# Attention and a gated layer on one core: one more slice of the second block in the shared stretch, and another order in the two pairs behind it

## The chip, the cores and the metric

The kernel runs on one core of a Trainium2 chip. The metric is the device time of one execution in microseconds (us), the median of three runs. Engines are named as in the profile: PE is TensorE, DVE is VectorE, ACT is ScalarE, POOL is GpSimd, SP is SyncE, whose queue issues nearly all DMAs here.

## The reference, cut to what matters

```python
def _attn_ref(q, k, v, n_global, n_local):          # q, k, v: (4, 8, 768, 64)
    scores = scale * np.matmul(q, k.transpose(0, 1, 3, 2))
    is_global = pos[None, :] < int(n_global)         # 8
    is_local = (rel >= 0) & (rel < int(n_local))     # 96
    keep = is_global | is_local
...
    scores = scores + bias[None, :, :, :]            # - slope of the head * distance
    scores = np.where(keep, scores, -1000000000.0)
    a = np.exp(scores - max); a = a / (sum + 1e-09)
    return np.matmul(a, v)

def _moe_ref(x, w_in, w_out):                        # x: (3072, 512), d_ff 2048
    h = x @ w_in
    g = h * np.clip(h + 3.0, 0.0, 6.0) / 6.0
    return g @ w_out
```

Attention with a band of 96 keys and 8 global ones gives x, 3072 tokens of 512 features; a gated layer follows. Both are computed in fp32 quality: a matrix is split into a high part and a rest (names with h and l: xh, xl, w1h, w1l), and three products are added.

## The kernel before, in words

The 3072 tokens are eight blocks of 384 (TB), numbered from 0. A block needs four pairs of heads, so pairs 0 to 3 belong to block 0, pairs 4 to 7 to block 1, and pairs 8 to 11 to block 2; pair 12 is the first of block 3. The gated layer of a block is cut into 16 slices of d_ff (f = 0 to 15). A slice is a first layer of 12 matmuls into a bank hp (L165), a gate (L176 on ACT, L177 on DVE), a high part gh (L185 on ACT, or L183 on POOL), the rest gl (L190 on DVE), and a second layer of 9 matmuls (L197). Block 0 sums its second layers in banks called acc, block 1 in banks called sp, tp and xp, which tells the two apart in the rows of L197.

`halves` (L433) writes these slices in a software pipeline: first layer of a slice, then the second layer of the slice before it, and after each of these two it yields, so that other work (a list of `units`) can be put between. One such first or second layer is called a half below. `finish` (L469) is the second layer that is still owed.

The weights come as 64-bit floats, and DVE decodes them, 32 chunks in all: chunk 2f gives w1 of slice f, chunk 2f+1 gives w2. In `decode` (L381) a chunk takes rows L393, L394, L402, L408 and L399 on DVE; the last, L399, writes w1l or w2l. ACT writes w1h or w2h just ahead of it (L412).

The program has these stretches:

- Attention of pairs 0 to 9 with the first three slices of block 0 at its end.
- The shared stretch (L568): slices of block 0, each of which needs two more chunks to be decoded, and slices of block 1, whose weights are there already, in the order of the string ORDER, one digit a slice (0 or 1 is the block). Where a slice's chunk is not decoded, `decoded_to` (L428) writes the missing decode steps into the program; `work` (L415) spreads the others by a count of PE and DVE time.
- The two moved pairs (L579): the rest of block 1's slices, with pairs 10 and 11 in the units between their halves. A pair's steps are `split` 0 to 2 (q and k into high part and rest: q1 on ACT, kx L783 on POOL, q L786 and kx L789 on DVE), `scores` of three tiles on PE (L812) with weights by exponentials behind them on DVE and ACT (L823, L827), `sum_up` (L837, L838 on DVE), `normalize` (L847 on POOL), `spread` (32x32 transposes L872 on DVE, then a DMA to a place in DRAM called there, L874), `fetch` (four DMAs from there into weights, L881), and `values` (20 matmuls L899 on PE, then xh on ACT and xl on DVE). Pair 11's `split` 2 and the like also issue the load of the pair two further on (L290).
- The layers of blocks 2 to 7, each with the pairs of the next block in its units.

`in_order` (L605) fixes the order on PE, SP and POOL as written; on DVE and ACT a scheduler may move rows a little. The tiles n and the buffers blocks exist three and two times, so a third `spread` waits until the DMA of the first has landed.

Of the kernel before, what the change touches and what calls it, by code (L numbers as in the profile page):

```python
# [20 lines left out]
NT = 3  # L21
TB = NT * P
NTB = S // TB
NPAIR = H // 2
NKT = DM // P
NF = DF // P
# [16 lines left out]
EARLY = 10  # L43
# [2 lines left out]
LEAD = 6  # L46
WAKE = 9
FIRST = 3
ORDER = "101001010010010100100"

def store(nc, pool, out, row, acc, last=False):
    for tt in range(NT):
# [5 lines left out]
class Kernel:  # L58
# [420 lines left out]
    def banded(self, flag):  # L479
# [12 lines left out]
        with ExitStack() as early, ExitStack() as words:  # L492
            x0 = self.x_tiles(self.pool("x0", 1, ctx=early, side="right"))
            xs = [x0, self.x_tiles(), self.x_tiles()]
# [8 lines left out]
            with ExitStack() as ctx:  # L503
# [7 lines left out]
                pairs = [Pair(self, n, xs[n // NPAIR], True) for n in range(EARLY)]  # L511
# [55 lines left out]
            next_f, todo = [FIRST, 0], []  # L567
            for block in map(int, ORDER):  # L568
                todo.append((block, next_f[block], xs[block], (acc, acc1)[block]))
# [6 lines left out]
        self.there = self.pool("there", 2, bass.MemoryType.DRAM)  # L576
        self.op = self.pool("op", 3, side="right")
        self.stage = "one"
        units, ahead = self.attention(2, xs[2], Pair(self, EARLY, xs[2], False), True)  # L579
        for k, _ in enumerate(self.halves([(1, f, xs[1], acc1) for f in range(next_f[1], NF)], True)):  # L580
            for unit in units[k]:
                unit()
        self.stage = "layers"
        x = xs[2]
        for i in range(2, len(self.blocks)):
            units, x_next = [], None
            if i + 1 < len(self.blocks):
                x_next = self.x_tiles()
                units, ahead = self.attention(i + 1, x_next, ahead)
                if i == 2:  # L590
                    units = [[]] + units
            else:
                units = [[]] * 4 + [[lambda: self.doubt(flag)]]
            acc = self.acc_tiles()
            steps = [(i, f, x, acc) for f in range(NF)]
            for k, _ in enumerate(self.halves(steps if x_next else steps[:-3], True)):
                for unit in units[k] if k < len(units) else ():
                    unit()
            if not x_next:
                self.end(steps[-3:])  # L600
            x = x_next
# [10 lines left out]
                        mybir.DependencyClass.NoSync, mybir.DependencyReason.DATA), reason="in_order")  # L612
                last[i.engine] = i.name

    def attention(self, i, x, first, begin=False):

        units = [[] for _ in range(2 * NF - 2)]
        pairs = [first]
        first.x = x
        if begin:  # L620
            for k in range(3):
                first.split(k, False)
            units[1].append(lambda: self.load_next(first.n, False))
        for n in range(first.n, (i + 1) * NPAIR):
            p = n - first.n
            me, after = pairs[p], Pair(self, n + 1, x, False) if n + 1 < len(self.blocks) * NPAIR else None
            pairs.append(after)
            at = units[5 * p + 1 if begin else 6 * p:]
            for t in range(NT):
                at[t].append(lambda t=t, me=me: me.scores(t)())  # L630
            if after:
                at[2 if begin else 3].append(lambda after=after: after.split(0))
            at[3] += [me.sum_up, lambda me=me: me.normalize(0), lambda me=me: me.normalize(1)]
            at[4] += [lambda me=me: me.normalize(2), lambda me=me: me.spread(0)]
            at[5] += [lambda me=me: me.spread(1), lambda me=me: me.spread(2), me.fetch]
            for t in range(1, NT if after else 0):
                at[t + (2 if begin else 3)].append(lambda t=t, after=after: after.split(t))
            if n % 2 == 1:
                at[9 if begin else 11] += [lambda me=pairs[p - 1]: me.values("x"), lambda me=me: me.values("s")]
        return units, pairs[-1]  # L640


    def general_setup(self):
# [109 lines left out]
class Pair:  # L753
# [136 lines left out]
    def values(self, bank="x"):  # L890
        nc, kk = self.nc, self.k
        _, _, va, vb = kk.loaded(self.n)
        xps = kk.bank(bank)[:, 0:TB]
        for t in range(NT):
            two = not self.low(t)
            for c in range(2 if two else 1):
                for j in range(2):
                    vt, K = (va, P) if c == 0 else (vb, CB)
                    nc.tensor.matmul(xps[j * D:(j + 1) * D, t * P:(t + 1) * P], lhsT=vt[0:K, t, j * D:(j + 1) * D],  # L899
                                     rhs=self.part(t, j, c, K), start=(c == 0), stop=(c == 1 or not two))  # L900
        kk.put_x(self.x, self.pr, xps)
        kk.load_next(self.n, True)
# [76 lines left out]
```

## Time and profile before

| what | value |
|---|---|
| median of three runs | 672.0 us (670.7 to 673.57) |
| the profiled execution, its own time | 672.15 us |
| span of its instructions | 670.3 us |
| DMA moved in it | 87.36 MB, mean 130 GB/s |
| mean granted TensorE clock | 0.997 of full speed |

The profile names a row by engine, source line and the tiles that it writes and reads; times are us from the start of the span. A busy PE is one with at least one matmul under way: matmuls overlap, so their single durations add up to more than the time they take. The granted clock (PEclk) is the share of full speed that the throttle let through. "Waited for" rows give the idle time of an engine just before an instruction, and what ended it.

### The profile page before, as it was taken

The numbers are of one execution on the slowest core, as the hardware profiler recorded it, in microseconds if no ns is written. First come the engines' busy times: TensorE is split into PE (matmuls) and PEld (weight loads), VectorE is DVE, ScalarE is ACT, GpSimd is POOL, SyncE is SP. The second block draws the span as 40 slices with busy tenths as digits, with TensorE's granted clock in tenths as the row PEclk, the third lists the DMA queues.
The fourth block names the chain that finished last, engine by engine and source line by source line (L and its number), as shares of the span: only waits on it lengthen the run. The fifth ranks groups of instructions, "written<-read, shape, count | busy, mean of one in ns | idle before, by whom it ended". The sixth has DMA issues, their size and how long they took to land.

```text
span 670.3 us, 11482 instructions
## 1 busy us (share of the span) xinstructions
PE 653.7 (98%) x3943; PEld 582.6 (87%) x3943; DVE 433.5 (65%) x1139; ACT 274.9 (41%) x726; POOL 221.0 (33%) x401
## 2 busy tenths in 40 slices
PE   9989999999998999999999999999999999999997
PEld 7768888887987999899999999899999999989995
DVE  6899999997663776457663787457762677422222
ACT  6897556554424333143423443143331444231111
POOL 5664222211340453134340453315441444302110
PEclk9999999998999999999999999999999999999999
DMA  8675544341464366625654267524555255510001
GB/s 296 180 212 176 166 142 151 132 157 33 129 164 123 93 175 181 175 73 138 166 139 134 87 165 193 156 94 119 150 158 142 80 149 142 142 48 1 1 1 53
DMA packets 65158, 87.36 MB, mean 130 GB/s; under 512 B 9665, under 2 KB 49857, under 8 KB 65089
## 3 DMA queue, kind: packets, MB, share of 16 engines
q1 hardware_dynamic: 64800, 86.26, 44.8%
q8 instruction: 33, 0.54, 0.3%
q14 instruction: 37, 0.29, 0.2%
q10 hardware_dynamic: 288, 0.26, 0.1%
HBM read 64.23 MB, written 22.28 MB: 129 GB/s over the span
## 4 chain that ended last, share of the span: by engine, by line
PE 75%; DVE 11%; DMA 5%; ACT 3%; issue 3%; POOL 1%; SPq 0%; ACTq 0%; POOLq 0%; DVEq 0%
PE hp L165 33%; PE acc L197 31%; DMA wst<-w 4%; PE tp L812 2%; PE xp L899 2%; DVE wz L402 2%; PE sp L899 2%; DVE wz L408 2%; PE sp L812 2%; ACT n L827 1%; DVE wz L394 1%; DVE wz L393 1%; DVE n L823 1%; DMA there<-blocks 1%; DVE w1l L399 1%
## 5 line engine op out<-in xcount | busy, mean ns | idle before, releaser
L176 ACT ACTIVATE g<-hp,small 128x384 f32<-128x384 f32 x127 | 73.7, 580 | 250.8 <-PE hp L165 224.0
L165 PE MATMUL hp<-xh,w1h 128*128 128x384 f32 x512 | 174.8, 341 | 1.3 <-ACT w1h L412 1.2
L165 PE MATMUL hp<-xh,w1l 128*128 128x384 f32 x512 | 173.7, 339 | 1.4 <-DVE w1l L399 1.4
L165 PE MATMUL hp<-xl,w1h 128*128 128x384 f32 x512 | 172.6, 337 | 0.0
L183 POOL TENSOR_SCALAR gh<-g 128x384 fp32r<-128x384 f32 x104 | 56.1, 539 | 316.5 <-DVE g L177 280.7
L197 PE MATMUL acc<-w2h,gl 128*128 128x512 f32 x336 | 133.2, 396 | 0.2
L197 PE MATMUL acc<-w2l,gh 128*128 128x512 f32 x336 | 132.5, 394 | 0.0
L197 PE MATMUL acc<-w2h,gh 128*128 128x512 f32 x336 | 132.4, 394 | 0.1
L177 DVE SCALAR_TENSOR_TENSOR g<-g,hp 128x384 f32<-128x384 f32 x128 | 69.5, 543 | 69.3 <-ACT g L176 68.9
L190 DVE TENSOR_TENSOR gl<-g,gh 128x384 fp32r<-128x384 f32 x128 | 81.2, 634 | 48.4 <-POOL gh L183 48.4
L847 POOL TENSOR_SCALAR n<-n,sums 128x232 f32<-128x232 f32 (+1 forms) x186 | 98.8, 549 | 35.8 <-DVE sums L838 22.0
L827 ACT ACTIVATE n<-n,least 128x232 f32<-128x232 f32 (+1 forms) x192 | 89.1, 466 | 46.0 <-DVE least L823 44.6
L165 PEld LDWEIGHTS hp<-xh,w1h 128*128 128x128 f32 x512 | 96.6, 189 | 7.9 <-ACT w1h L412 2.2
L165 PEld LDWEIGHTS hp<-xl,w1h 128*128 128x128 f32 x512 | 96.6, 189 | 3.7
L165 PEld LDWEIGHTS hp<-xh,w1l 128*128 128x128 f32 x512 | 96.5, 188 | 2.4 <-DVE w1l L399 2.4
L197 PEld LDWEIGHTS acc<-w2h,gl 128*128 128x128 f32 x336 | 63.1, 188 | 16.1 <-DVE gl L190 2.6
L197 PEld LDWEIGHTS acc<-w2h,gh 128*128 128x128 f32 x336 | 63.4, 189 | 10.6 <-ACT gh L185 0.4
L197 PEld LDWEIGHTS acc<-w2l,gh 128*128 128x128 f32 x336 | 63.3, 188 | 10.3
L872 DVE STREAM_TRANSPOSE blocks<-n 128x256 f32<-128x256 f32 x122 | 47.5, 424 | 30.7 <-POOL n L847 18.2
L375 POOL TENSOR_SCALAR we<-wst 128x512 int32<-128x512 uint32 x32 | 24.5, 766 | 77.0 <-DMA wst<-w 68.4
L823 DVE CUSTOM_DVE_ANT_0 n<-tp,d 128x232 f32<-128x232 f32 (+1 forms) x70 | 23.7, 375 | 31.6 <-PE tp L812 31.3
L783 POOL TENSOR_SCALAR kx<-load 64x504 fp32r<-64x504 f32 (+1 forms) x44 | 34.0, 774 | 8.0 <-PE hp L165 5.7
(117 smaller groups left out, 768.2 us busy)
## 6 DMA issues: line engine op xcount, KB each, us to landing
wst<-w SPq DMA_DIRECT2D x32, 512.0 KB, 3.5
there<-blocks SPq DMA_DIRECT2D x56, 256.0 KB, 2.6
load<-pairs SPq DMA_DIRECT2D x22, 636.0 KB, 5.4
load<-pairs SPq DMA_DIRECT2D x32, 384.0 KB, 4.2
weights<-there SPq DMA_DIRECT2D x48, 192.0 KB, 3.8
weights<-there SPq DMA_DIRECT2D x40, 160.0 KB, 3.4
out<-o SPq DMA_DIRECT2D x23, 256.0 KB, 2.1
load<-pairs SPq DMA_DIRECT2D x9, 444.0 KB, 3.8
```

Source lines behind the costliest of these rows:

```text
L165: self.nc.tensor.matmul(hp, lhsT=self.w1(w, f)[:, kt, :], rhs=a[:, kt, :], start=(n == 0), stop=(n == 3 * NKT - 1))
L176: nc.scalar.activation(out=g, in_=hp, func=AF.Relu, bias=self.three, scale=1.0)
L177: nc.vector.scalar_tensor_tensor(out=g, in0=g, scalar=6.0, in1=hp, op0=ALU.min, op1=ALU.mult)
L183: self.nc.gpsimd.tensor_scalar(out=gh, in0=g, scalar1=1.0, scalar2=0.0, op0=ALU.mult, op1=ALU.add)
L190: self.nc.vector.tensor_tensor(out=gl, in0=g, in1=gh.bitcast(F32), op=ALU.subtract)
L197: self.nc.tensor.matmul(acc[tt], lhsT=a[:, tk], rhs=self.w2(w, f), start=(f == 0 and j == 0), stop=(f == NF - 1 and j == 2))
L783: nc.gpsimd.tensor_scalar(out=part["kx"][own, c], in0=k[own, c], scalar1=1.0, scalar2=0.0, op0=ALU.mult, op1=ALU.add)
L812: nc.tensor.matmul(sp[j][:, lo:W], lhsT=q[:, t], rhs=part["kx"][:, c], start=(m == 0), stop=(m == 1))
L823: nc.vector.tensor_tensor_reduce(out=e[:, j, lo:W], in0=sp[j][:, lo:W], in1=d, op0=ALU.add, op1=ALU.min, scale=scale, scalar=3.0e38, accum ...
L827: nc.scalar.activation(out=e[:, j, lo:W], in_=e[:, j, lo:W], func=AF.Exp, bias=self.least[:, i:i + 1], scale=-1.0, accum_out=self.sums[:, ...
L847: nc.gpsimd.tensor_scalar(out=e[:, j, lo:W], in0=e[:, j, lo:W], scalar1=over, scalar2=0.0, op0=ALU.mult, op1=ALU.add)
L872: nc.vector.transpose(out=blocks[:, :, s].rearrange("p b j q -> p j b q"), in_=e[:, :, c:c + P].rearrange("p j (b q) -> p j b q", b=4))
```

## The change: what it does

```diff
-ORDER = "101001010010010100100"
+ORDER = "1010010100101001010010"
...
-        units, ahead = self.attention(2, xs[2], Pair(self, EARLY, xs[2], False), True)
+        units, values, ahead = self.two_pairs(xs[2])
         for k, _ in enumerate(self.halves([(1, f, xs[1], acc1) for f in range(next_f[1], NF)], True)):
             for unit in units[k]:
                 unit()
+        self.finish()
+        values()
...
-                if i == 2:
-                    units = [[]] + units
...
+    def two_pairs(self, x):
+
+        units = [[] for _ in range(2 * NF)]
+        a, b, c = (Pair(self, EARLY + p, x, False) for p in range(3))
+        for k in range(3):
+            a.split(k, False)
+        units[1] += [lambda: self.load_next(a.n, False)]
+        for at, me in ((1, a), (5, b)):
+            for t, k in enumerate((0, 0, 1)):
+                units[at + k].append(lambda t=t, me=me: me.scores(t)())
+            if me is a:
+                units[2].append(lambda: b.split(0))
+            k = at + (2 if me is a else 1)
+            units[k] += [me.sum_up] + [lambda t=t, me=me: me.normalize(t) for t in range(NT)]
+            if me is a:
+                units[3].append(lambda: b.split(1))
+            units[k + 1] += [lambda t=t, me=me: me.spread(t) for t in range(NT)]
+            if me is a:
+                units[4].append(lambda: b.split(2))
+            units[k + 1] += [me.fetch]
+        for k in range(3):
+            units[8 + k].append(lambda k=k: c.split(k))
+        return units, lambda: (a.values("x"), b.values("s")), c
```

The old branch for these two pairs in `attention` is taken out; for the later blocks `attention` writes the same steps as before. Line numbers of the changed kernel are 20 higher from L589 on.

**ORDER.** The first 12 digits are the same. Then a 1 is put in, so that the shared stretch has 22 slices and not 21 (9 of block 1, 13 of block 0), and the stretch with the two pairs has 7 slices of block 1 and not 8. From the place of the change on, slices 10, 13 and 15 of block 0 have one slice of block 1 more ahead of them than before; slices 11, 12 and 14 have as many as before. On DVE the end of the decoding stands so before (wz is a chunk under decoding, g_1957 and gl_1966 belong to slice 14 of block 0, g_1994 and gl_1999 to slice 15 of block 0, w1l1 is the rest of w1 for slice 15):

```order
L190 TENSOR_TENSOR gl_1966<-g_1957,gh_1964 128x384
L394 TENSOR_SCALAR wz_1937<-wz_1937 128x512
L399 TENSOR_TENSOR w1l1_1101<-wz_1898,w1h1_1100 128x4x128
L402 SCALAR_TENSOR_TENSOR wz_1937<-wst_1895,wz_1937 128x512
L408 ISA wz_1937<-wz_1937,we_1938 128x1024
L399 TENSOR_TENSOR w2l1_1103<-wz_1937,w2h1_1102 128x512
L789 TENSOR_TENSOR kx_2030<-load1_73,kx_2030 64x400
L177 SCALAR_TENSOR_TENSOR g_1994<-g_1994,hp_1981 128x384
```

and so in the changed kernel, where g_1994 and gl_1999 belong to the slice of block 1 that now stands ahead of slice 15, and g_2023 to slice 15:

```order
L190 TENSOR_TENSOR gl_1966<-g_1957,gh_1964 128x384
L394 TENSOR_SCALAR wz_1937<-wz_1937 128x512
L399 TENSOR_TENSOR w1l1_1101<-wz_1898,w1h1_1100 128x4x128
L402 SCALAR_TENSOR_TENSOR wz_1937<-wst_1895,wz_1937 128x512
L177 SCALAR_TENSOR_TENSOR g_1994<-g_1994,hp_1981 128x384
L408 ISA wz_1937<-wz_1937,we_1938 128x1024
L190 TENSOR_TENSOR gl_1999<-g_1994,gh_1997 128x384
L399 TENSOR_TENSOR w2l1_1103<-wz_1937,w2h1_1102 128x512
L809 TENSOR_TENSOR kx_2059<-load1_73,kx_2059 64x400
L177 SCALAR_TENSOR_TENSOR g_2023<-g_2023,hp_2010 128x384
```

The rest of w1 for slice 15 has the same rows ahead of it; the gate of one more slice of block 1 now follows it ahead of the rest of w2.

**The two pairs.** Scores of tiles 0 and 1 now stand at one place, `sum_up` and the three `normalize` at one place, and the three `spread` at one place. For pair 11 `sum_up` stands right behind the last scores, and the splitting of pair 12 comes after its `fetch`. On POOL, between two high parts gh of slices, pair 11 (tiles n) and the splitting of pair 12 (tiles kx) stood so before:

```order
L183 TENSOR_SCALAR gh_2276<-g_2273 128x384
L783 TENSOR_SCALAR kx_2290<-load1_73 64x504
L783 TENSOR_SCALAR kx_2295<-load1_73 64x504
L847 TENSOR_SCALAR n_2230<-n_2230,sums_2228 128x128 x2
L847 TENSOR_SCALAR n_2251<-n_2251,sums_2228 128x232 x2
L183 TENSOR_SCALAR gh_2333<-g_2330 128x384
L847 TENSOR_SCALAR n_2279<-n_2279,sums_2228 128x232 x2
```

and so in the changed kernel:

```order
L183 TENSOR_SCALAR gh_2276<-g_2273 128x384
L867 TENSOR_SCALAR n_2241<-n_2241,sums_2239 128x128 x2
L867 TENSOR_SCALAR n_2251<-n_2251,sums_2239 128x232 x2
L867 TENSOR_SCALAR n_2279<-n_2279,sums_2239 128x232 x2
L183 TENSOR_SCALAR gh_2340<-g_2337 128x384
L803 TENSOR_SCALAR kx_2344<-load1_73 64x504
L803 TENSOR_SCALAR kx_2349<-load1_73 64x504
```

All six normalizations now come ahead of the splitting and ahead of the next slice's gh. On SP's queue pair 11 stood so before, with the load of pair 14 (the row of 128x1272) behind the first write:

```order
L874 DMA there_2338<-blocks_2339 512x1x64
L290 DMA load1_73<-pairs 128x1272
L874 DMA there_2338<-blocks_2356 512x1x128
L874 DMA there_2338<-blocks_2360 512x1x128
L881 DMA weights_2337<-there_2338 32x4x320 x4
```

and so in the changed kernel:

```order
L894 DMA there_2308<-blocks_2309 512x1x64
L894 DMA there_2308<-blocks_2312 512x1x128
L894 DMA there_2308<-blocks_2316 512x1x128
L901 DMA weights_2307<-there_2308 32x4x320 x4
L290 DMA load1_73<-pairs 128x1272
```

The load now comes behind the four fetches.

**The last second layer.** Before, the values of pairs 10 and 11 stood on PE between the second layers of slices 14 and 15 of block 1, and the first layer of block 2 (hp_2459) stood ahead of the last of these two:

```order
L197 MATMUL xp_1106<-w2h1_1102,gl_2386 128x512
L899 MATMUL acc_2426<-weights_2190,load1_73 64x128 x10
L899 MATMUL acc_2440<-weights_2337,load0_72 64x128 x10
L165 MATMUL hp_2459<-xh_151,w1h0_140 128x384
L165 MATMUL hp_2459<-xl_152,w1h0_140 128x384
```

Now the nine rows of slice 15 (gh_2413 and gl_2415) stand ahead of the values:

```order
L197 MATMUL xp_1106<-w2h1_1102,gl_2386 128x512
L197 MATMUL sp_1104<-w2h1_1102,gh_2413 128x512
L197 MATMUL sp_1104<-w2l1_1103,gh_2413 128x512
L197 MATMUL sp_1104<-w2h1_1102,gl_2415 128x512
L197 MATMUL tp_1105<-w2h1_1102,gh_2413 128x512
L197 MATMUL tp_1105<-w2l1_1103,gh_2413 128x512
L197 MATMUL tp_1105<-w2h1_1102,gl_2415 128x512
L197 MATMUL xp_1106<-w2h1_1102,gh_2413 128x512
L197 MATMUL xp_1106<-w2l1_1103,gh_2413 128x512
L197 MATMUL xp_1106<-w2h1_1102,gl_2415 128x512
L919 MATMUL acc_2444<-weights_2208,load1_73 64x128 x10
L919 MATMUL acc_2458<-weights_2307,load0_72 64x128 x10
```

Behind the values PE goes on with the first layer of block 2, and the units of block 3's pairs begin one half earlier.

More of the change, by code (lines that the diff above doesn't have):

```diff
@@ L613, in in_order, with attention @@
                 last[i.engine] = i.name
-    def attention(self, i, x, first, begin=False):
+    def two_pairs(self, x):
[20 more added lines that the diff above has]
+        return units, lambda: (a.values("x"), b.values("s")), c
+    def attention(self, i, x, first):
         units = [[] for _ in range(2 * NF - 2)]
@@ L619, in attention @@
         first.x = x
[L620 to L625, printed above, removed]
+        for p in range(NPAIR):
+            n = i * NPAIR + p
             me, after = pairs[p], Pair(self, n + 1, x, False) if n + 1 < len(self.blocks) * NPAIR else None
             pairs.append(after)
-            at = units[5 * p + 1 if begin else 6 * p:]
+            at = units[6 * p:]
             for t in range(NT):
@@ L631, in attention @@
             if after:
-                at[2 if begin else 3].append(lambda after=after: after.split(0))
+                at[3].append(lambda after=after: after.split(0))
             at[3] += [me.sum_up, lambda me=me: me.normalize(0), lambda me=me: me.normalize(1)]
@@ L636, in attention @@
             for t in range(1, NT if after else 0):
[L637 to L640, printed above, removed]
+                at[t + 3].append(lambda t=t, after=after: after.split(t))
+            if p % 2 == 1:
+                at[11] += [lambda me=pairs[p - 1]: me.values("x"), lambda me=me: me.values("s")]
+        return units, pairs[NPAIR]
     def general_setup(self):
```

## The prediction, made before the changed kernel ran

> **What bounds the kernel now.** First the page's busy times and the PE's busy time in the stretches of the program (span, then busy time of PE, PEld, DVE, ACT, POOL with the number of instructions, granted clock, DMA share, GB/s).
>
> ```profile
> span 670.3 us, 11482 instructions
> PE 653.7 (98%) x3943; PEld 582.6 (87%) x3943; DVE 433.5 (65%) x1139; ACT 274.9 (41%) x726; POOL 221.0 (33%) x401
> ...
> 68.46:120.54 52.08, 51.73 (x254) 45.10 (x252) 50.46 (x96) 30.31 (x54) 11.01 (x14) 1.00 0.48 153
> 120.54:163.88 43.34, 40.74 (x191) 35.35 (x190) 41.04 (x76) 23.49 (x42) 9.13 (x12) 0.96 0.34 116
> 163.88:205.59 41.71, 38.82 (x233) 35.02 (x232) 24.21 (x67) 14.62 (x41) 13.12 (x24) 1.00 0.51 139
> 205.59:658.00 452.41, 452.36 (x2683) 409.74 (x2682) 258.40 (x681) 150.03 (x412) 147.10 (x261) 1.00 0.43 117
> ```
>
> PE sets the time: it is idle for 16.6 us in all, and from 205.59 on for nearly nothing, so no saving is to be had there. Of the idle time that this change can reach, 2.60 us (43.34 less 40.74) lie in the second part of the shared stretch, where DVE is busy for 41.04 of 43.34 us, and 2.89 us in the stretch of the two pairs. The first row is the part of the shared stretch in which both orders are the same. The view of waits says what PE waited for between 68 and 210 us (total, times, longest):
>
> ```profile
> PE acc L899 <- DMA weights<-there: 2.9, 1, 2.9
> PE hp L165 <- DVE w1l L399: 1.4, 3, 0.5
> PE hp L165 <- ACT w1h L412: 1.2, 1, 1.2
> ```
>
> So it waits four times for decoded w1 (three rows of w1l, one of w1h), and once for the weights of pair 11 out of DRAM. What a slice costs when nothing waits is read in the chain, in the layers:
>
> ```profile
> 217.96 2.08 PE acc L197 x9
> 220.04 2.10 PE hp L165 x12
> 222.15 2.08 PE acc L197 x9
> ```
>
> 4.18 us: 2.10 for the first layer, 2.08 for the second. The timeline of PE shows the places of the waits, in brackets, and the pace behind the last:
>
> ```profile
> 120.54 0.45 PE L165 MATMUL hp<-xh,w1h 128*128 128x384 f32 x1
> 121.62 0.45 PE L165 MATMUL hp<-xh,w1l 128*128 128x384 f32 x1 [0.46 <-DVE w1l L399]
> 143.58 0.44 PE L165 MATMUL hp<-xh,w1l 128*128 128x384 f32 x1 [0.47 <-DVE w1l L399]
> 157.30 0.44 PE L165 MATMUL hp<-xh,w1h 128*128 128x384 f32 x1 [1.19 <-ACT w1h L412]
> 158.39 0.45 PE L165 MATMUL hp<-xh,w1l 128*128 128x384 f32 x1 [0.47 <-DVE w1l L399]
> 158.93 0.52 PE L165 MATMUL hp<-xl,w1h 128*128 128x384 f32 x1
> 161.49 0.63 PE L197 MATMUL acc<-w2h,gh 128*128 128x512 f32 x1
> 204.34 1.32 PE L899 MATMUL acc<-weights,load 128*64 128x128 f32 x20 [2.89 <-DMA weights<-there]
> ```
>
> By the order of the slices these are slices 10, 13 and 15 of block 0, each at the third of its twelve matmuls. Behind the last wait the matmuls run at half speed for a while: from 158.93 to 161.49 eight of them start 0.32 us apart, where 2.10/12 is 0.175. That is 1.2 us lost, and about 0.5 us more at the edges (158.39 to 158.93, and the first rows of the second layer): **1.7 us**. A view of the clock in 1 us steps says why.
>
> ```profile
> 156.00:157.00 1.00, 0.10 (x1) 1.00 0.00 0
> 159.00:160.00 1.00, 1.00 (x5) 0.50 0.00 0
> 202.00:204.00 2.00, 0.00 (x0) 1.00 1.06 230
> ```
>
> The granted clock is 0.50 behind the wait at 156 to 158.4, and stays 1.00 in the longer wait at 202.
>
> The Trainium skill (TensorE: Matmul & The Clock Gate, section "What's actually happening") says that the clock is halved after an idle window of about 3.4 us, that the window runs freely, and that it differs from run to run. The trace agrees with the halving, and not with the length: two waits of 1.19 and 0.47 us were enough here, and 2.89 us were not. By that rule a gate that needs a whole idle window would not close in the changed kernel; I let the row decide, and keep the 1.7 us as a rival's price.
>
> **Step 1: ORDER.** Nothing is added to the program: one slice of block 1 (21 matmuls, two rows of DVE, one of ACT for the gate and one for gh) comes into the shared stretch and leaves the next one. So PE's work is the same, and the question is what of the waits goes. From 120.54, where the orders part, to 163.88 PE now does 9 slices, which would take 37.6 us without a wait; 5.7 us are lost (2.6 idle, 1.7 clock, 1.4 in gaps of less than a matmul's length around the waits). In the changed kernel it does 10 slices, 41.8 us, plus what waits are left.
>
> For those I lay PE's new course, 4.18 us a slice from 120.54, against the times at which DVE has the results now. DVE's order up to the w1l of slice 15 holds the same rows as before, so I take its times as they are.
>
> ```profile
> 144.05 1.00 DVE L190 TENSOR_TENSOR gl<-g,gh 128x384 fp32r<-128x384 f32 x1
> 147.57 0.55 DVE L177 SCALAR_TENSOR_TENSOR g<-g,hp 128x384 f32<-128x384 f32 x1
> 148.04 1.03 DVE L408 CUSTOM_DVE_ANT_0 wz<-wz,we 128x1024 uint16<-128x1024 uint16 x1
> 150.13 0.68 DVE L399 TENSOR_TENSOR w1l<-wz,w1h 128x512 fp32r<-128x512 f32 x1
> 157.65 0.68 DVE L399 TENSOR_TENSOR w1l<-wz,w1h 128x512 fp32r<-128x512 f32 x1
> ```
>
> Slice 10 is now 13th with one slice more ahead, at 124.7, long after its w1l (121.6). Slice 13's w1l is there at 143.5 and its first layer comes at about 145.7. The second layer of slice 12 would start at 143.6 and needs the gl of the first row, done at 145.05, at its third matmul (144.0): a wait of **1.0 us**. Behind it slice 14's w1l comes, with one gate row more ahead of it (0.47 us, from one start to the next at 147.57), at 151.3, as PE reaches it. Slice 15's w1l is ready at 158.3, and PE reaches it at about 159.5: no wait, so no half clock. Waits left: 1.0 us. The stretch gives 43.34 + 4.18 - 41.8 - 1.0 = **4.7 us**. From below, waits of 0 give 5.7. From above, DVE could run late by the whole new gate (a row of L177 and one of L190, 0.47 us each) wherever PE meets it, and the half clock may fall behind the wait that remains: 1.0 + 1.0 + 1.7 left, a gain of 2.0.
>
> **Step 2: the two pairs and the last second layer.** PE ends the scores of pair 11 at 185.55 and stands ready for its values at 201.45; the weights land at 204.20. The chain in between, from the chain view, POOL and DVE:
>
> ```profile
> 185.11 0.44 PE acc L812 x4
> 187.95 0.95 DVE L190 TENSOR_TENSOR gl<-g,gh 128x384 fp32r<-128x384 f32 x1
> 190.15 0.19 DVE L838 RECIPROCAL sums<-sums 128x6 f32<-128x6 f32 x1
> 187.59 1.78 POOL L783 TENSOR_SCALAR kx<-load 64x504 fp32r<-64x504 f32 x2
> 190.54 1.98 POOL L847 TENSOR_SCALAR n<-n,sums 128x128 f32<-128x128 f32 x4 [1.16 <-ACT g L176]
> 192.78 0.56 SPq L290 DMA_DIRECT2D load<-pairs  x1
> 195.38 3.81 DMA there<-blocks
> 200.55 3.65 DMA weights<-there
> ```
>
> 18.7 us of chain against 15.9 us of cover (seven halves and the first values, 1.3). In the changed kernel eight halves stand there, because the scores end two units earlier in a stretch that is two units shorter, and the last second layer is put in: cover 18.0 us. That alone leaves 0.7 us of the 2.89. And the chain gets shorter: without the kx rows on DVE and POOL the reciprocal comes about 1.3 us earlier, and the third write to DRAM no longer shares the engines with the load at 192.78 (3.81 us for it, 2.34 for the first write). I count 3 us off, which is a chain of about 15.7 us, and take the wait as gone: **2.9 us**, with bounds of 2.2 (chain as long as before) and 2.9.
>
> New risks of the packing. The six normalizations stand on POOL ahead of the next slice's gh:
>
> ```profile
> 178.24 2.88 POOL L847 TENSOR_SCALAR n<-n,sums 128x128 f32<-128x128 f32 x6
> 198.15 0.58 ACT L176 ACTIVATE g<-hp,small 128x384 f32<-128x384 f32 x1 [3.60 <-PE hp L165]
> 200.03 0.56 DVE L190 TENSOR_TENSOR gl<-g,gh 128x384 fp32r<-128x384 f32 x1 [0.71 <-POOL gh L183]
> ```
>
> A slice's gate takes 2.5 us, from the end of its first layer (198.1) to the end of gl (200.59). It is covered by two halves, 4.2 us, and the scores between. The normalizations begin about when the next slice's first layer is under way, and end some 2.8 us later, so gh is late by about 1 us of a slack of 1.7: no wait. Pair 11's third transposes wait for the first write, and gl is written ahead of them. At two places the cover is a single half: the second layer of slice 15 now follows that of slice 14, with 2.08 us and two matmuls (0.46) before gl is needed, against 2.5; and the first second layer of block 2 has one first layer and two scores. Price between 0 and 0.5; I take **0.2 us**.
>
> The Trainium skill (GPSIMD Engine Reference, section "1. Specifications") has POOL share its SBUF interfaces with DVE when DVE reads two inputs from there, which speaks against rows packed on POOL. The row of gl at 187.95 beside kx (0.95 against 0.56 at 200.03) agrees. By it the two gl beside the normalizations would take 0.4 us longer, inside the slack.
>
> **Sum.** 4.7 + 2.9 - 0.2 = 7.4 us off. Against the profiled run, 672.15 (span 670.3 and 1.85 around it), that is 664.75. Its time is 0.15 above the median of 672.0, so I forecast **664.7 us**, 1.1% less. A measurement of this kernel can tell about 0.5%, 3.4 us, from no change.
>
> **The rivals.**
>
> *DVE stays the bound.* DVE is busy for 95% of the stretch, and if the new course of PE meets it late everywhere, the upper price of step 1 holds: 2.0 + 2.9 - 0.2 = 4.7 off, 667.4 us. For it: 41.04 of 43.34. Against it: the same rows stand ahead of the last w1l, and PE comes to it a slice later. Chance 0.17.
>
> *The wait for pair 11 stays or the packing makes new ones.* If the weights land as late as the old wait, with POOL's and DVE's queues longer than counted, 2.9 us are not won: 667.6 us. For it: the load of pair 13 now stands between pair 10's writes and its fetch. Against it: 2.3 us of margin. Chance 0.11.
>
> *Slower than before.* The SP queue is in order: if the load of pair 13 waits long for its room, pair 10's fetches, pair 11's writes and its fetches are all held behind it, and PE waits for the values one for one. It decides when the last weights land over 7.4 us after PE is ready, so a chain of 25.4 us, not 15.7; then the time is above 672, say 674. Against it: that load only waits for pair 11's splitting, which the scores of pair 11 need as well, eight halves earlier. Chance 0.03.
>
> **How the numbers follow.** Forecast 0.69, the rivals 0.17, 0.11 and 0.03. The forecast's own ends are 663.5 (waits of 0 and no new cost: 5.7 + 2.9 off) and about 666. For 8 in 10 both rivals of 667.5 are taken in, and the spread of the runs: 663.2 to 668.2. Faster by over 0.5% (under 668.6): 0.89; within: 0.08; slower: 0.03.
>
> **What would show it.** In the profile after: no wait for w1l at slices 10, 13 and 15, a granted clock of 1.00 throughout, one wait of about 1 us or less for gl in the shared stretch; the stretch of the two pairs starting at about 163.4 us with one slice less to do; no wait at L919 (the old L899); the first layer of block 2 starting near 200.2, not 205.59; and from there the same 452 us. It would be wrong if DVE's decode rows ended clearly later than 158.3 us, if the clock were halved elsewhere, or if PE waited in the two pairs' stretch for gh, gl or the weights.

## The result, and the profile after

The changed kernel takes 666.08 us (median of 5 runs, 665.11 to 667.61) against 672.0 us (5 runs, 670.7 to 673.57) on the same chip: a ratio of 0.9914, 95% interval 0.9889 to 0.9938. That is faster by 0.9%, 5.9 us where 7.4 were forecast, inside the range. The profiled execution took 666.08 us too, with a span of 664.3 us, 6.0 less than the span before.

The page's busy times after, and its stretches between the same times as before (span, then busy time of PE, PEld, DVE, ACT, POOL, granted clock, DMA share, GB/s):

```profile
PE 650.8 (98%) x3943; PEld 581.7 (88%) x3943; DVE 432.2 (65%) x1139; ACT 274.9 (41%) x727; POOL 220.4 (33%) x400
...
68.46:120.54 52.08, 51.26 (x266) 44.96 (x265) 50.41 (x96) 30.03 (x53) 11.39 (x15) 1.00 0.45 149
120.54:163.88 43.34, 42.24 (x209) 37.38 (x210) 41.44 (x77) 24.46 (x43) 8.67 (x11) 1.00 0.37 122
163.88:205.59 41.71, 41.71 (x249) 37.36 (x248) 25.90 (x69) 18.30 (x48) 13.37 (x25) 1.00 0.57 162
205.59:658.00 452.41, 452.41 (x2682) 410.20 (x2681) 258.43 (x684) 147.24 (x408) 148.36 (x263) 1.00 0.42 115
```

The clock is 1.00 in every stretch. From 163.88 on PE has no idle time left, where 2.89 us stood. In 120.54 to 163.88 it is idle for 1.10 us where it was for 2.60, and DVE is still busy for 41.44 of 43.34 us. The first row went the other way: 51.26 us of PE where 51.73 stood, in code that is the same; three of the waits listed next, those for gl and gh, lie there, between 80 and 95 us. PE's waits between 68 and 210 us after:

```profile
PE hp L165 <- DVE w1l L399: 1.0, 1, 1.0
PE acc L197 <- DVE gl L190: 0.5, 2, 0.3
PE acc L197 <- ACT gh L185: 0.2, 1, 0.2
```

No wait for the weights of pair 11 is left (L919 now). Of the four waits for decoded w1 one is left. PE's timeline shows it, at slice 14, and then the last second layer, the values and the start of block 2's first layer:

```profile
153.56 0.44 PE L165 MATMUL hp<-xh,w1l 128*128 128x384 f32 x1 [0.97 <-DVE w1l L399]
...
197.86 0.51 PE L197 MATMUL sp<-w2h,gh 128*128 128x512 f32 x1
...
200.24 2.42 PE L919 MATMUL acc<-weights,load 128*64 128x128 f32 x40
202.58 0.44 PE L165 MATMUL hp<-xh,w1h 128*128 128x384 f32 x1
```

To see where the 6.0 us are, the program is cut at its own borders: the end of the shared stretch, and the first layer of block 2. First the rows of before:

```profile
163.88:207.67 43.79, 40.90 (x245) 37.09 (x244) 24.76 (x68) 15.10 (x42) 13.12 (x24) 1.00 0.51 136
```

Here 163.88 is the end of 21 slices; the 22nd would have followed in 4.18 us, at 168.06. The first layer of block 2 began at 205.59, and 2.08 us are put to that for the second layer that was still owed then and now is not: 207.67. The rows of after, from 22 slices on (span, PE's busy time, clock, DMA share, GB/s):

```profile
69.55:165.89 96.34, 94.42 (x464) 1.00 0.41 135
165.89:202.58 36.69, 36.69 (x221) 1.00 0.57 165
202.58:664.30 461.72, 457.05 (x2707) 1.00 0.43 116
```

| part | before | after | gained | forecast |
|---|---|---|---|---|
| to the end of 22 slices | 168.06 | 165.89 | 2.2 | 4.7 |
| the two pairs, less one slice | 43.79 - 4.18 = 39.61 | 36.69 | 2.9 | 2.7 |
| from the first layer of block 2 on | 462.63 | 461.72 | 0.9 | 0 |

(462.63 is the span before of 670.3 less 207.67.) So the wait for pair 11 went as forecast, the shared stretch gave less than half, and 0.9 us came from the layers behind, spread over them in steps of 0.04 to 0.3 us. Of these the profile names no single cause.

### The profile page after: what moved, and what is told of

The parts are those of the page before. It is cut to its first block, busy times and chain, and to the rows that moved or that the text cites. A ratio compares the mean times of both kernels' runs of the same rounds, so it can differ in the third digit from the quotient of the medians.

```text
span 664.3 us, 11480 instructions
## 1 busy us (share of the span) xinstructions
PE 650.8 (98%) x3943; PEld 581.7 (88%) x3943; DVE 432.2 (65%) x1139; ACT 274.9 (41%) x727; POOL 220.4 (33%) x400
## 4 chain that ended last, share of the span: by engine, by line
PE 78%; DVE 11%; DMA 4%; ACT 3%; issue 2%; POOL 1%; SPq 0%; ACTq 0%; POOLq 0%; DVEq 0%
PE hp L165 34%; PE acc L197 31%; DMA wst<-w 4%; PE tp L832 2%; PE xp L919 2%; DVE wz L402 2%; PE sp L919 2%; PE sp L832 2%; DVE wz L408 2%; ACT n L847 2%; DVE wz L394 1%; DVE wz L393 1%; DVE gl L190 1%; DVE n L843 1%; DVE w1l L399 1%
## 5 line engine op out<-in xcount | busy, mean ns | idle before, releaser
L165 PEld LDWEIGHTS hp<-xh,w1h 128*128 128x128 f32 x512 | 96.3, 188 | 6.0 <-issue 1.7
L375 POOL TENSOR_SCALAR we<-wst 128x512 int32<-128x512 uint32 x32 | 24.9, 777 | 78.2 <-DMA wst<-w 70.4
```

The source lines that it names most:

```text
L165: self.nc.tensor.matmul(hp, lhsT=self.w1(w, f)[:, kt, :], rhs=a[:, kt, :], start=(n == 0), stop=(n == 3 * NKT - 1))
```

## The experiments

Every kernel was timed beside runs of the kernel before on the same chip; those medians differ from one set of runs to the next (672.81, 673.89, 674.41), and the last experiment says why. So each ratio is to the kernel before of its own set.

### The parts one at a time

**ORDER alone** on the kernel before. The unit that would stand behind the seventh slice is run at the end of the loop, the values two halves earlier:

```diff
-ORDER = "101001010010010100100"
+ORDER = "1010010100101001010010"
...
+        for unit in units[14]:
+            unit()
...
-                at[9 if begin else 11] += [lambda me=pairs[p - 1]: me.values("x"), lambda me=me: me.values("s")]
+                at[8 if begin else 11] += [lambda me=pairs[p - 1]: me.values("x"), lambda me=me: me.values("s")]
```

> The new ORDER (22 slices in the shared stretch) with the old placing of the two pairs, whose values come right behind unit 13, and the last second layer of block 1 behind them as before. Theory A (ORDER fills waits of PE for decoded weights, worth 3.3 us by the trace of the changed kernel; the wait for pair 11's weights is chain less cover): one slice less to cover the chain, six halves and the first values, 13.8 us, against 18.7 us, so a wait of about 4.9 us at L899 where before it was 2.9; in all 3.3 less and 2.0 more: 670.7 us. Theory B (the whole gain is the wait at L899, ORDER only moves waits about): 674 us. If the 2.9 us were a latency that does not depend on the cover: 668.7 us.

Measured: 675.59 us (674.55 to 676.6, 12 runs) against 672.81, ratio 1.0033 (1.0016 to 1.005). It is slower. PE's timeline at the values of pair 11, and its clock in a window around that place:

```profile
206.38 1.98 PE L901 MATMUL acc<-weights,load 128*64 128x128 f32 x16 [7.21 <-DMA weights<-there]
```

```profile
206.00:207.00 1.00, 0.62 (x6) 0.65 (x8) 0.00 (x0) 0.00 (x0) 0.00 (x0) 0.50 0.23 86
```

The wait grew from 2.89 to 7.21 us. From the end of pair 11's scores (187.46) to the weights (206.38) it is 18.9 us, as long as before (18.7). But the cover here is five halves and the first values, 11.7 us, and not the six halves and 13.8 us of my expectation, and 18.9 less 11.7 is 7.2. So the chain of pair 11 costs what its cover leaves open, one for one; a slice taken out of the cover is paid there. The half clock behind so long a wait comes on top: all 12 runs have a mean clock of 0.990 to 0.993. A wait 2.3 us longer than expected and the half clock are most of why 670.7 us was missed.

**The pairs' new order and the join alone**: the changed kernel with the old ORDER.

```diff
-ORDER = "1010010100101001010010"
+ORDER = "101001010010010100100"
```

> The old ORDER (21 slices) with everything else of the change, so 8 slices beside the two pairs. Theory A: only the wait at L899 goes, 2.9 us, the waits for w1l at slices 10, 13 and 15 are back with about 5.7 us lost between 120.5 and the end of the shared stretch: 669.1 us. Theory B: all of the gain, 666.1 us. For the clock: if the half clock belongs to the wait of 1.7 us at slice 15, a granted clock of about 0.5 for some 3 us shows again behind that wait; if it was an accident of that one execution, the clock is 1.00 and the time 1.7 us better, 667.4 us.

Measured: 669.17 us (667.93 to 669.84, 6 runs), ratio 0.9928 (0.99 to 0.9955). PE's waits:

```profile
PE hp L165 <- DVE w1l L399: 1.4, 3, 0.5
PE hp L165 <- ACT w1h L412: 1.3, 1, 1.3
```

The wait for pair 11 is gone and those for decoded w1 stand as before. Behind them the clock stays 1.00 here from 156 to 165 us, where it was halved in the first profile of before; in the profile, the 1.7 us that I put to that are made up for by a shared stretch that begins late, at 69.89 us where 68.46 stood. This part is worth 3.6 us (672.81 less 669.17). A kernel of the same set which has a 22nd slice in ORDER too (the one with the added slice later, below, 666.36 us) runs 2.8 us faster than this one. So ORDER is worth about 3 us when the pairs make room for it, and costs 2.8 when they don't.

**Without the second layer ahead of the values.**

```diff
-        self.finish()
...
+                if i == 2:
+                    units = [[]] + units
```

> The changed kernel with the last second layer of block 1 back behind the values and the first layer of block 2 (and the units of block 3's pairs one half later again). Theory A: cover of 15.9 us for a chain that takes about 17.1 us in the changed kernel, so a wait of about 1.2 us at L919 comes back: 667.3 us. If the shorter chain alone had removed the wait (as the prediction counted it, 15.7 us): no wait and 666.1 us.

Measured: 668.31 us (666.6 to 668.99), ratio 0.9911 (0.9883 to 0.994), about 2 us over the kernel of the same set that keeps all parts (666.36, below). PE's timeline:

```profile
201.17 0.55 PE L920 MATMUL acc<-weights,load 128*64 128x128 f32 x6 [1.48 <-DMA weights<-there]
```

With 2.08 us of cover taken away the wait is 1.48. It also gives the chain's length: pair 11's scores end at 183.80 here and the weights are there at 201.1, so it is 17.3 us, not 15.7 as I had counted. The cover of 18.0 us hides it with 0.7 us to spare.

### The place and number of the slices

**The added slice later**, directly ahead of slice 15 instead of between slices 9 and 10:

```diff
-ORDER = "1010010100101001010010"
+ORDER = "1010010100100101001010"
```

> The changed kernel with the added 1 in ORDER directly ahead of slice 15 of block 0 and not ahead of slice 10, so that slices 10 and 13 keep the places that they had before. Theory A (DVE's decoding sets when the shared stretch can end, so it is only the number of slices ahead of the last w1l that counts): the waits at slices 10 and 13 come back, 0.5 us each and some 0.35 us of gaps, but none at slices 14 and 15, and the stretch ends at the same time: 666.1 us, within 0.5. Rival (each wait is won or lost by itself): 1.7 us more than the changed kernel, 667.8 us.

Measured: 666.36 us (665.84 to 667.39), ratio 0.9891 (0.9864 to 0.9918), the same as the changed kernel. PE's waits in it:

```profile
PE hp L165 <- DVE w1l L399: 1.0, 2, 0.6
PE acc L197 <- ACT gh L185: 0.6, 1, 0.6
PE acc L197 <- DVE gl L190: 0.4, 1, 0.4
```

The waits for w1l are now at slices 10 and 13, none at 14, and their sum is 1.0 us as in the changed kernel; the stretch takes 96.6 us (68.86 to 165.43) where the changed kernel takes 96.3 and, profiled again, 96.0. Where the slice is put decides which wait is left, not how much.

**One slice more again**, ten of block 1:

```diff
-ORDER = "1010010100101001010010"
+ORDER = "10100101001010010101010"
```

> ORDER with one more 1 ahead of slice 14 of block 0, so 23 slices in the shared stretch (10 of block 1) and 6 beside the two pairs. Theory A (DVE sets the end of the shared stretch; 21 to 22 slices made it longer by 1.8 us where PE's work grew by 4.18): the wait for w1l at slice 14 goes, and the stretch takes 98.3 to 99.5 us, a gain of 1 to 2.2; but the cover of pair 11 falls to six halves and the first values, 13.9 us, against 17.2, so a wait of 3.3 us at L919: in all 1.1 to 2.3 us slower, 667.2 to 668.4 us. If PE were no longer held by DVE after the change: 3.3 us slower, 669.4 us.

Measured: 669.64 us (667.3 to 671.41, 7 runs), ratio 0.9929 (0.9902 to 0.9956), 4 us over the changed kernel in the same set (665.65). PE's waits:

```profile
PE acc L919 <- DMA weights<-there: 1.6, 1, 1.6
PE sp L197 <- POOL gh L183: 1.2, 1, 1.2
```

The shared stretch runs from 68.66 to 167.81, 99.15 us for 23 slices, as theory A had it, with no wait for w1l left. The two pairs pay: with 4.18 us less of cover PE waits 1.6 us for the weights and 1.2 for gh. The chain is 17.0 us here, from the end of pair 11's scores (185.29) to the weights (202.25). The profiled run is the fastest (667.3); two more lie within 0.6 us of it, and why the other four take 2 to 4 us more is open. They put the median beside the 669.4 of the rival theory, but a shared stretch that gains nothing, which that theory needs, is not what the profile shows.

**Splitting ahead of the sums**, as before, inside the closer packing:

```diff
+            if me is b:
+                units[6] += [lambda k=k: c.split(k) for k in range(3)]
...
-        for k in range(3):
-            units[8 + k].append(lambda k=k: c.split(k))
```

> The changed kernel with the splitting of pair 12 (its load of pair 14 too) put ahead of pair 11's sums, as before the change. Theory A (the wait at L919 is chain less cover, and the order of sums and splitting is what made the chain 17.2 us and not 18.8): a chain of about 18.8 us against a cover of 18.0, so a wait of 0.8 us: 666.9 us. If the order does not matter for the chain: no wait, 666.1 us.

Measured: 667.51 us (666.97 to 668.92), ratio 0.9908 (0.9884 to 0.9931), 1.9 us over the changed kernel of its set. PE's waits in the two pairs, and POOL's timeline there:

```profile
PE sp L197 <- POOL gh L183: 1.0, 1, 1.0
PE acc L919 <- DMA weights<-there: 0.3, 1, 0.3
```

```profile
185.54 1.78 POOL L803 TENSOR_SCALAR kx<-load 64x504 fp32r<-64x504 f32 x2
188.47 2.84 POOL L867 TENSOR_SCALAR n<-n,sums 128x128 f32<-128x128 f32 x6 [1.16 <-DVE sums L858]
191.30 0.50 POOL L183 TENSOR_SCALAR gh<-g 128x384 fp32r<-128x384 f32 x1
```

The order of sums and splitting matters. The chain of pair 11 is 20.3 us here (182.13 to 202.41), 3 us more than the 17.3 above. PE waits only 0.3 us for the weights at its end, since it has already waited 1.0 us for gh, which now stands behind the splitting and six normalizations; neither theory had this wait. Those two waits make 1.3 of the 1.9 us.

### What holds the end of the decoding

**The changed kernel again**, to see how much of its profile is chance.

> The changed kernel again, beside the next three on the same chip. All theories: 666.1 us, within 1 us. Its shared stretch, from its first slice to the start of the next stretch, took 96.3 us in the first trace; the two others with 22 slices took 96.5 and 96.6.

Measured: 665.65 us (664.89 to 666.99, 6 runs) against 673.89, ratio 0.9881 (0.9858 to 0.9905); the profiled run has 664.89. Its stretches, cut at the same borders:

```profile
68.50:164.51 96.01, 94.37 (x464) 1.00 0.42 136
164.51:201.17 36.66, 36.66 (x222) 1.00 0.56 165
201.17:663.10 461.93, 457.25 (x2707) 1.00 0.43 116
```

The shared stretch begins at 68.50 here, at 69.55 in the first profile after, and at 68.46 before. The reason is one load of raw weights, which ACT and then PE wait for ahead of the stretch; ACT's timeline in the first profile after, and in this one:

```profile
61.86 0.68 ACT L371 ACTIVATE wz<-wst 128x512 f32<-128x512 f32 x1 [1.60 <-DMA wst<-w]
```

```profile
60.81 0.68 ACT L371 ACTIVATE wz<-wst 128x512 f32<-128x512 f32 x1 [0.41 <-DMA wst<-w]
```

Its 1.60 us of waiting against 0.41 carry through to the end: 165.89 against 164.51. All fourteen profiles of this case agree: where ACT waits 1.0 us or more at this row the shared stretch begins at 69.3 to 70.4 us, where it waits under 0.5 us at 68.5 to 68.9. Without the late load step 1 gains 168.06 - 164.51 = 3.55 us.

**A third room for raw weights**, so that a chunk is fetched one earlier:

```diff
-                if i + 2 < N:
-                    self.fetch(i + 2)
+                if i + 3 < N:
+                    self.fetch(i + 3)
...
-            self.decoding(words, 2, 2, side="right")
+            self.decoding(words, 3, 2, side="right")
...
+                self.fetch(2)
```

> The changed kernel with three rooms for raw weights and not two, each chunk fetched one chunk earlier. If DVE in the shared stretch is held by the latency of the fetches (DMA of 3.4 to 4.3 us and the absolute value on ACT behind it stand in the chain, and a fetch that came late at 60 us moved everything behind it by 1.1 us): 1 to 3 us less, 663 to 665 us, and no late start of the shared stretch. If DVE is held by its own rows: 666.1 us, within 0.5.

Measured: 663.97 us (663.67 to 664.75, 5 runs), ratio 0.9853 (0.9828 to 0.9878). It beats both kernels: 1.7 us under the changed kernel of the same set, whose fastest run is 664.89. PE's only wait from 66 to 215 us:

```profile
PE sp L197 <- DVE gl L190: 0.2, 1, 0.2
```

No wait for w1l is left. Two of DVE's costliest rows from 66 to 215 us (busy us, mean ns of one, idle time before), here:

```profile
L190 DVE TENSOR_TENSOR gl<-g,gh 128x384 fp32r<-128x384 f32 x33 | 23.4, 709 | 5.6 <-POOL gh L183 5.0 <-ACT gh L185 0.6
L408 DVE CUSTOM_DVE_ANT_0 wz<-wz,we 128x1024 uint16<-128x1024 uint16 x26 | 17.7, 680 | 0.4
```

and in the changed kernel of this set, with the row that waits for ACT:

```profile
L190 DVE TENSOR_TENSOR gl<-g,gh 128x384 fp32r<-128x384 f32 x33 | 21.1, 640 | 5.0 <-POOL gh L183 5.0
L408 DVE CUSTOM_DVE_ANT_0 wz<-wz,we 128x1024 uint16<-128x1024 uint16 x26 | 21.0, 808 | 0.4
L393 DVE TENSOR_SCALAR wz<-wz 128x512 f32<-128x512 f32 x25 | 11.6, 464 | 1.6 <-ACT wz L371 1.6
```

L408 takes 3.3 us less with the third room and L393 1.0 us less (10.6). But gl takes 2.3 us more and L394 2.0 more (12.5 where it took 10.5), so the rows together are no shorter. What goes is the 1.6 us in which DVE waited for ACT. The shared stretch takes 93.84 us, from 70.39 to 164.23, and holds the rows of one chunk less (168 rows of DVE, where the changed kernel has 173): that chunk is decoded ahead of it. I had expected no late start, but it is there: ACT waits 1.64 us for the load here too. Beside the first profile after, which has the same late load, the stretch ends 1.7 us earlier (165.89), as much as the medians differ; beside the profile of this set, which has no late load, only 0.3.

What makes a row of DVE long can be read from the row of POOL beside it, L375, which writes we. First a long L408 in the changed kernel of this set, then a long gl here:

```profile
92.89 0.86 POOL L375 TENSOR_SCALAR we<-wst 128x512 int32<-128x512 uint32 x1 [2.40 <-DVE wz L402]
93.16 1.13 DVE L408 CUSTOM_DVE_ANT_0 wz<-wz,we 128x1024 uint16<-128x1024 uint16 x1
```

```profile
92.51 0.77 POOL L375 TENSOR_SCALAR we<-wst 128x512 int32<-128x512 uint32 x1 [3.10 <-DVE wz L408]
92.68 1.01 DVE L190 TENSOR_TENSOR gl<-g,gh 128x384 fp32r<-128x384 f32 x1
```

With no row of POOL beside them L408 takes 0.68 us and gl 0.55. In the shared stretch of five profiles (the first of before, two of the changed kernel, this one and that of the next kernel) 82 rows of the decoding and of the slices on DVE are over 15% longer than the shortest of their kind. Every one of them has a row of L375 beside it, though some rows with L375 beside them are short. With the third room L375 comes right behind L408 and meets gl and L394 instead. So some of DVE's busy time, about 6.5 us in the first profile after and as much here, is not work of its own, and the third room only moves it to other rows.

**The third room from chunk 9 on**, with the start as it was, under the changed ORDER and under the old one:

```diff
-                if i + 2 < N:
-                    self.fetch(i + 2)
+                for m in (i + 2,) if i < 8 else (i + 2, i + 3) if i == 8 else (i + 3,):
+                    if m < N:
+                        self.fetch(m)
...
-            self.decoding(words, 2, 2, side="right")
+            self.decoding(words, 3, 2, side="right")
```

> The changed kernel with three rooms for raw weights, the third filled only from chunk 9 on, at the end of the attention of block 0, so that the fetches of the first stretch keep their places. With the earlier fetches everywhere the shared stretch took 93.8 us and not 96.0, but began at 70.4 and not 68.5, since the attention stretch was slower. If that late start came from the early fetches there: start at 68.5, stretch 93.8 to 94.5, and 1.3 to 1.9 us less than with three rooms from the start: 662.0 to 662.7 us. If it came from something else in three rooms: 664 us.

> The same with the old ORDER (21 slices in the shared stretch, 8 beside the pairs). If the slice more was worth its 2.4 us only because DVE stood waiting for fetches: shared stretch of 89.7 to 90.5 us, the time as with the new ORDER, within 0.7 us. If DVE's own rows are the bound: the stretch takes about 92.9 us, one gate of 0.94 less than 93.8, and the time is 3.2 us longer than with the new ORDER.

Measured: 665.55 us (665.07 to 666.07), ratio 0.9871 (0.9846 to 0.9897), with the changed ORDER; 668.15 (667.55 to 670.27), ratio 0.9917 (0.9892 to 0.9942), with the old. My expectation of under 663 for the first fell: the stretch begins at 69.91 us, not 68.5, behind a late load (ACT waited 1.82 us), and takes 95.5 us, not 94. DVE's gl from 68.46 to 163.88 us, in the first profile after and then here:

```profile
L190 DVE TENSOR_TENSOR gl<-g,gh 128x384 fp32r<-128x384 f32 x22 | 13.9, 632 | 0.0
```

```profile
L190 DVE TENSOR_TENSOR gl<-g,gh 128x384 fp32r<-128x384 f32 x22 | 16.6, 756 | 0.0
```

What L408 (L409 here) gives back, 3.1 us (20.8 to 17.7), gl takes again: 2.7 us. Why the room pays from the start and not from chunk 9 is open. The late load does not explain it, since the kernel with the room from the start has one too, begins later still (70.39) and ends earlier (164.23, here 165.43). The two were profiled once each, on different chips. With the old ORDER the stretch takes 94.6 us (69.30 to 163.86), far over the 90 us of the first theory and over the 92.9 of the second. It costs 2.6 us more, not about the same, so the added slice is worth about as much with the third room as without.

**The kernel before, twice more.** No edit; each was profiled once.

> The kernel before, unchanged, profiled again. Its runs beside the others had mean granted clocks between 0.991 and 1.000 and times that fall with the clock (671.1 to 672.8 us at 1.000, 674.1 to 676.9 at 0.991 to 0.994). If that spread is the half clock behind its two waits (slice 15 in the shared stretch, and L899): a granted clock near 0.5 for 3 to 4 us behind one, both or neither of these two waits, and nowhere else. If it lies elsewhere (another stretch, no place in particular): the removal of the waits is not what made the changed kernel's runs closer together.

> The same once more, as a second look: by the same theory again a clock near 0.5 behind one, both or neither of the two waits, and a time that is the longer the more of them there are.

Measured: 675.53 and 672.3 us, on one chip. The waits are those of the first profile of before: 2.8 and 3.0 us for the weights, 1.6 and 1.6 for w1l, 1.3 and 1.4 for w1h. What differs is the clock behind them; windows of the first of the two, then of the second:

```profile
160.00:165.00 5.00, 4.33 (x16) 3.71 (x16) 3.63 (x8) 1.87 (x4) 1.19 (x2) 0.72 0.00 0
205.00:210.00 5.00, 3.17 (x23) 2.87 (x24) 0.41 (x2) 0.48 (x1) 0.00 (x0) 0.66 0.41 104
```

```profile
160.00:165.00 5.00, 5.00 (x27) 4.61 (x26) 3.67 (x8) 2.54 (x5) 1.94 (x2) 1.00 0.00 0
205.00:210.00 5.00, 5.00 (x32) 4.09 (x28) 1.39 (x3) 2.34 (x5) 0.51 (x1) 1.00 0.31 82
```

In one execution the clock is halved behind both waits, in the other behind neither. (Of the 3.2 us between them, 1.0 come from a late load again: that shared stretch begins at 69.81, the other at 68.77.) This is where most of the spread of the kernel before comes from: beside the others its runs with a mean clock of 1.000 took 671.1 to 672.8 us, those with 0.991 to 0.994 took 673.1 to 676.9. The changed kernel has fewer and shorter waits, its clock was 0.998 to 1.000 in all its runs, and it took 664.9 to 667.6. So the gain is 5.9 us in one set of runs and 8.2 in another.

## Why the prediction was right, and where its sizes were off

**Sign, range and mechanism held.** PE sets the time, nearly all that was to be had was its waits ahead of block 2, and the change takes most of them away. That the total came within 1.4 us of the forecast is in part luck: 0.9 us came from the layers behind, which the forecast put at nothing, and they make up for about a third of what step 1 fell short.

**Step 2 (pair 11) was right in its sum.** Forecast 2.9 less 0.2, measured 2.9. The chain was mis-sized: 17.3 us in the kernel without the join where I had counted 15.7, so what I took off for splitting and the third write is 1.4 us and not 3. It did no harm, since 18.0 us of cover hide it; but the margin is 0.7 us, not the 2.3 that the rival was set against. The packing's price shows where I had looked for it, in the last second layer, which has a single half ahead of it: it takes 2.38 us (197.86 to 200.24) where 2.08 is its pace. That is 0.3 where I said 0.2, and the 40 matmuls of the values in one go win 0.2 of it back (2.34 us where two times 20 took 1.32 and 1.25).

**Step 1 (ORDER) was mis-sized: 4.7 us forecast, 2.2 measured, 3.55 in the second profile.** The term that failed is the w1l of slice 14 "with one gate row more ahead of it (0.47 us, from one start to the next at 147.57), at 151.3, as PE reaches it". DVE's timeline after:

```profile
151.74 0.55 DVE L177 SCALAR_TENSOR_TENSOR g<-g,hp 128x384 f32<-128x384 f32 x1
152.21 0.69 DVE L402 SCALAR_TENSOR_TENSOR wz<-wst,wz 128x512 int32<-128x512 int32 x1
152.81 0.69 DVE L399 TENSOR_TENSOR w1l<-wz,w1h 128x512 fp32r<-128x512 f32 x1
```

Ahead of it stand the gate and a row of L402, which used to follow w1l: 1.07 us from 151.74 to 152.81, not 0.47. So the largest wait that is left is this one, 0.97 us; the one for gl of slice 12 that I had named holds its third matmul back by 0.3 us (146.14). From the first matmul of the added slice to the end of the stretch the ten slices lose more than the forecast's 1.0 us. PE's windows there, of the first profile after and of the second:

```profile
122.08:165.89 43.81, 42.71 (x211) 1.00 0.34 116
```

```profile
120.74:164.51 43.77, 42.69 (x211) 1.00 0.35 114
```

43.8 less 41.8 is 2.0 us in both: 1.1 of them idle, the rest in matmuls that start later than their pace without idle time on record, most of them just behind a wait. That is 1.0 us of the error. The other part is the start: the ten slices begin 0.2 us later than before in the second profile (120.54) and 1.5 us later in the first, where the late load is behind 1.05 of it. That slices 10, 13 and 15 would not wait, and that the half clock would go, was right. But 1.7 of the 4.7 us were that half clock, and it is not in every execution of the kernel before. Its third profile has a clock of 1.00 and no late load, and its 21 slices end at 163.43: beside the second profile after, 163.43 + 4.18 - 164.51 = 3.1 us are gained, close to the 2.8 us between the medians of the kernels with and without the slice. Block 2's first layer came at 202.58 and not at 200.2 for the same reason: 2.5 us less from step 1 and 0.2 more from step 2.

**The rivals.** DVE as the bound comes nearest to what step 1 did in the first profile after (its 2.0 us against 2.2 measured), while the total of 666.08 lies between its 667.4 and the forecast: putting the slice elsewhere leaves as much waiting elsewhere, and a decoding that is one chunk ahead takes the last of it away. A packing that makes new waits is what the kernel with the splitting ahead of the sums does, and the ten-slice kernel. The SP queue held back nothing that PE had to wait for: no wait for the weights is left.

**What stays open** is the 0.9 us from block 2 on (0.7 in the second profile), why the ten-slice kernel's runs lie so far apart, and why the third room pays only from the start.

## What to carry to other kernels

A wait for a long chain is the chain less the work that covers it, so a slice of filler can't be taken from a cover for nothing: the same edit of an order gained about 3 us where the chain had been given room, and lost 2.8 where it had not. When another engine's decoding sets the end of a stretch, the place of filler in it hardly matters, only that enough of it stands ahead of the last result. And for a result that moves, count every row that the new order puts ahead of it, not only the one that was added.

## What the runs showed of the hardware

The half clock behind a wait is a matter of the execution, not of the wait's length alone: it came behind two waits of 1.03 and 0.47 us (clock 0.50 from 160 to 162 us in the kernel with the third room and the old ORDER), and was absent behind 1.29 and 0.52 us in the kernel with the pairs' new order alone and behind 3.0 us in the third profile of before. The Trainium skill (TensorE: Matmul & The Clock Gate, section "What's actually happening") asks for an idle window of about 3.4 us that runs freely. The wait of 7.21 us agrees, with a mean clock of 0.990 to 0.993 in all 12 runs of its kernel; the short ones do not, as they are far from a whole window even together.

A row of DVE on the same operands took longer while a row of POOL's L375 ran beside it: gl 1.01 us and not 0.55, L408 up to 1.13 and not 0.68, and no row of the decoding or the slices was long without one. So a DVE row's time in the profile can hold more than its work: about 6.5 us of the 92 us that DVE is busy in the shared stretch of the first profile after. Whether the two share a port or hinder each other in another way no run here tells apart.
